# Soft-capped attention and two feed-forward layers on one core: the attention's blocks in batches of four

## The chip, the core and the metric

One core of one Trainium2 chip runs the whole program. Times are device microseconds (us) of one execution; a kernel's time is the median of its runs.

## The reference

Two batches of 12 heads, 448 positions, head width 64, all in fp32; then two feed-forward layers on the 896 rows of width 768.

```python
scores = (q @ k.T) / sqrt(64)
scores = cap * tanh(scores / cap)
attn = exp(scores - max(scores))
attn = attn / (sum(attn) + 1e-9)
x = attn @ v                               # 896 x 768 over heads
x = relu(x @ w_in) ** 2 @ w_out            # 768 -> 2048 -> 768
out = silu(x @ w2_in) @ w2_out
```

## The kernel before, in words

All products run on the matrix engine (PE), tanh and exp on ACT, sums and copies on DVE, some conversions on POOL. SP issues nearly all loads and stores. Every engine works through its own list in the order in which the program was written; the program is written by hand, and only semaphores hold an engine up.

**The attention** (`attention_bounded`, line 582) handles the 24 heads as 12 pairs, and two pairs (A and B) as a *quad* m, from 0 to 5. The 448 keys of a pair are three blocks of 128 and a rest of 64; the rests of A and B are put together in one block. So a quad has seven blocks, `A0 A1 A2 C B0 B1 B2`, where C is the block of rests, and there are 42 blocks in all. A block passes through:

- *scores* (`scores`, line 616): PE writes keys by queries for two heads into a pair of PSUM banks (`bank2`, two pairs in turn). ACT takes tanh out of it into a tile e, of which there are eight in turn (line 630); an exp in place follows (line 726). The pair of banks is free after the tanh.
- *values* (`values`, line 632): PE multiplies e with v and adds up in one bank per pair of heads, px.
- *add* (`add`, line 649): DVE adds the blocks of a pair to a tile total. The half of C that belongs to A is added when C comes, and B's half when B1 comes.

After B2, PE adds the totals up over the keys (`add_up`, line 663, into a bank `sum`); DVE copies them (`evacuate_sums`), SP moves them into another layout, DVE inverts them (`invert`, lines 693 and 694), SP stores them (line 695) and fetches them back, broadcast over the partitions (`fetch`, line 701), and DVE multiplies the copied px with them (`normalise`, line 706), after which POOL splits the result into two fp16 parts for the feed-forward. The last two pairs have another way: their sums are made on all partitions (`add_up_pair`, line 673) and inverted at full width (`last_sums`, line 709).

PSUM has eight banks: four for px, sums and what follows (`bank`), four as two pairs for scores.

**The order** is the loop from line 721 over batches `groups[h]` of two blocks, 21 of them. In iteration h come: the scores and tanhs of batch h, its exps, the loads that its blocks call for; the DVE copies of px that batch h-2 completed; adds and values of batch h-1; then, if batch h-2 had a B2, the sum of that quad and its copy. The rest of that quad's work hangs on a list `todo`: the inversion one iteration later, the fetch two, the two normalises four and six iterations later. Between iterations 5 and 16 one step per iteration prepares weights of the feed-forward (`ws.step`), and six weight loads stand at fixed iterations (`loads`, line 719).

**The feed-forward** follows at once. Its products (line 914) are ordered by a planner that interleaves the preparation of weights; its first products need the attention's pieces x0 in the order of the pairs. Its accumulators lie in the four banks that the scores had, and in the four others.

Of the kernel before, what the change touches and what calls it, by code (L numbers as in the profile page):

```python
# [8 lines left out]
F32 = mybir.dt.float32  # L9
BF16 = mybir.dt.bfloat16  # L10
# [5 lines left out]
ALU = mybir.AluOpType  # L16
# [10 lines left out]
def softcap_attention_relu2_silu(  # L27
# [48 lines left out]
    psum = ctx.enter_context(tc.tile_pool(name="psum", bufs=2, space=PSUM))  # L76

    dram = ctx.enter_context(tc.tile_pool(name="dram", bufs=1, space=bass.MemoryType.DRAM))

    def bank(name):  # L80
        return psum.tile([128, 512], F32, tag="p", bufs=4, name=name)

    def bank2(spool, name):
        return spool.tile([128, 2, 512], F32, tag="s", bufs=2, name=name)


    idle = work.tile([128, S], F32, tag="r", bufs=NR, name="idle")
    nc.vector.memset(idle[:, :128], 0.0)
    ib, ip = idle.bitcast(BF16), bank("idle")
    for _ in range(20):  # L90
        nc.tensor.matmul(ip[:, :256], lhsT=ib[:, :128], rhs=ib[:, :256], start=True, stop=True)


    cap = cap.rearrange("(a b) -> a b", a=1)
# [487 lines left out]
    def attention_bounded(att, spool, ws, x0):  # L582
# [22 lines left out]
        ex, total, px, sums, st, rb = {}, {}, {}, {}, {}, {}  # L605

        NQ = NP2 // 2
        blocks = [(m, x) for m in range(NQ) for x in ("A0", "A1", "A2", "C", "B0", "B1", "B2")]
# [1 line left out]
        def pair_of(m, x):  # L610
            return 2 * m + "AB".index(x[0])

        def head(j):
            return slice(64 * j, 64 * j + 64)

        def scores(m, x):
            sp = bank2(spool, f"s{m}_{x}")
            for j in range(2):
                for b in range(2) if x == "C" else (None,):
                    qk = pr.qk[pair_of(m, x) if b is None else 2 * m + b]  # L620
                    c = 3 if b is not None else int(x[1])
# [10 lines left out]
        def values(m, x):  # L632
            for i in (2 * m, 2 * m + 1) if x == "C" else (pair_of(m, x),):
                if i not in px:
                    px[i] = bank(f"px{i}")
            e = ex[m, x]
            for b in range(2) if x == "C" else (None,):
                for j in range(2):
                    i = pair_of(m, x) if b is None else 2 * m + b
                    v_m = pr.vt[i]  # L640
                    nc.tensor.matmul(  # L641
                        px[i][head(j), :S],
                        lhsT=v_m[:, 3 * j + int(x[1])] if b is None else pr.vc[m][head(b), j],
                        rhs=e[:, j] if b is None else e[head(b), j],
                        start=x == "A0" or b == 1,
                        stop=x == "B2" or b == 0,
                    )

        def add(m, x):
            e, i = ex[m, x], None if x == "C" else pair_of(m, x)  # L650
            if i == NP2 - 1:
                return
            if x in ("A1", "B1"):
                t = total[i] = att.tile([128, 2, S], F32, tag=f"total{x[0]}", bufs=2, name=f"total{i}")
                nc.vector.tensor_tensor(t, ex[m, x[0] + "0"], e, op=ALU.add)  # L655
            if x in ("A2", "B2"):
                nc.vector.tensor_tensor(total[i], total[i], e, op=ALU.add)  # L657
            if x in ("C", "B1"):
                b = int(x == "B1")
                t = total[2 * m + b][head(b)]  # L660
                nc.vector.tensor_tensor(t, t, ex[m, "C"][head(b)], op=ALU.add)  # L661

        def add_up(m):

            s = sums[m] = bank(f"sum{m}")
            for b in range(2):
                for j in range(2):
                    at = 32 * (2 * b + j)
                    nc.tensor.matmul(  # L669
                        s[at : at + 32, :S], lhsT=one[:, :32], rhs=total[2 * m + b][:, j], start=True, stop=True  # L670
                    )

        def add_up_pair(i, t, start=True, stop=True, part=slice(0, 128)):

            if start:
                sums["p", i] = bank(f"sump{i}")
# [28 lines left out]
        def normalise(i):  # L705
            nc.vector.tensor_tensor(cell(i), cell(i), rb.pop(i), op=ALU.mult)
            x0.now(i)
# [8 lines left out]
            return [a, b, c]  # L716

        todo, last = [], 2 * NQ - 2
        loads = {0: 0, 2: 1, 4: 2, 7: 3, 11: 4, 16: 5}
        groups = [blocks[n : n + 2] for n in range(0, len(blocks), 2)]  # L720
        for h in range(len(groups) + 1):
            if h < len(groups):
                for m, x in groups[h]:
                    scores(m, x)
                for m, x in groups[h]:
                    nc.scalar.activation(ex[m, x], ex[m, x], AF.Exp, scale=scale_c)  # L726
                for m, x in groups[h]:
                    if x in ("A0", "B0"):
                        i = pair_of(m, x)
                        if i + 2 < NP2:  # L730
                            pr.load_v(i + 2)
                    if x in ("A1", "C") and m + 1 < NQ:
                        pr.load(2 * m + 2 + (x == "C"))
            if h == 1:

                nc.vector.tensor_scalar(gcap, capt, -CAP_MAX, CAP_MAX, op0=ALU.max, op1=ALU.min)
                nc.scalar.activation(gcap, gcap, AF.Abs)
                nc.scalar.activation(gcap, gcap, AF.Exp, scale=-1.0)
                nc.vector.tensor_scalar(gcap, gcap, 1e-9 * ONE, None, op0=ALU.mult)
            older = groups[h - 2] if h > 1 else []  # L740
            for m, x in older:
                if x in ("C", "B2"):
                    evacuate(2 * m + (x == "B2"))
            for m, x in groups[h - 1] if h else []:
                add(m, x)
            for m, x in groups[h - 1] if h else []:
                values(m, x)
            for m, x in groups[h - 1] if h else []:
                if m == NQ - 1 and x in ("C", "B0", "B1", "B2"):
                    add_up_pair(  # L750
                        last + 1, ex[m, x], x == "C", x == "B2", head(1) if x == "C" else slice(0, 128)
                    )
                if m == NQ - 1 and x == "C":
                    add_up_pair(last, total[last])
            for m, x in older:
                if x == "B2":
                    add_up(m)
                    evacuate_sums(m)
                    todo.append((lambda m=m: invert(m), h + 1))
                    todo.append((lambda m=m: fetch(m), h + 2))  # L760
                    for b in range(2):
                        todo.append((lambda i=2 * m + b: normalise(i), h + 4 + 2 * b))
            if h in loads:
                ws.load_to(loads[h])
            for f, at in list(todo):
                if h >= at:
                    f()
                    todo.remove((f, at))
            if 5 <= h < 17:
                ws.step()  # L770
        for st_ in last_sums(last):
            st_.fn()
        for f, _ in todo:
            f()
        nc.scalar.activation(cell(last + 1), px.pop(last + 1)[:, :S], AF.Copy)
# [2 lines left out]
    def attention_general(att, spool, ws, x0):  # L778
# [8 lines left out]
        for i in range(NP2):  # L787
            pr.load(i)
            pr.load_whole_v(i)
            for j in range(2):  # L790
# [5 lines left out]
                    for a in ("mx", "nm", "sm", "rs")  # L796
                )
                for g in range(2):
                    sp = bank2(spool, f"sg{n}_{g}")
# [751 lines left out]
    def run(attention, tag, dt):  # L1551
        narrow = dt == F16
        power = POWER if narrow else dict.fromkeys(POWER, 0)
        with ExitStack() as pools:
# [96 lines left out]
```

## Time and profile before

| | |
|---|---|
| median of 3 runs | 499.09 us (498.02 to 499.17) |
| profiled execution | 498.42 us, of which the span from first to last instruction is 496.6 us |
| PE | 486.7 us busy, 98% |
| DVE | 404.5 us busy, 81% |
| ACT | 370.0 us busy, 75% |
| POOL | 31.2 us busy, 6% |
| PE's granted clock | 0.999 of full speed |
| chain that ended last | PE 94% |
| attention | from 5 us to 86.8 us of the span |

Busy time is the time in which an engine's instructions run. PE's is modelled at the ends, so 98% does not mean that its products run at their peak; that is why the lengths of single pieces and the waits are read below. The chain of work that ended last is followed back from the last instruction, at each step to what released it.

### The profile page before, as it was taken

Reading aid. Unit: us, or ns where it says so; the run is one execution under the profiler, and the core shown is the slowest. Engines: PE = TensorE matmul, PEld = TensorE weight load, DVE = VectorE, ACT = ScalarE, POOL = GpSimd, SP = SyncE. Lnnn points to the kernel's source line nnn. Section 1 sums busy time; section 2 is a strip of 40 time slices with the busy share of each in tenths; the row PEclk is TensorE's granted clock in tenths of the full one; section 3 lists DMA queues with packets and bytes.
Section 4 is the critical chain, followed back from the end, with each engine's and each line's share of the span. In section 5 each row is a group of like instructions: output and inputs, shape, how many; then the busy total and the mean of one; then the engine's idle time right before and its main releaser. Section 6 shows DMA issues by size and latency. Waiting matters only on the chain.

```text
span 496.6 us, 7168 instructions
## 1 busy us (share of the span) xinstructions
PE 486.7 (98%) x2581; PEld 235.1 (47%) x2581; DVE 404.5 (81%) x787; ACT 370.0 (75%) x594; POOL 31.2 (6%) x33
## 2 busy tenths in 40 slices
PE   8999999999999999999999998999999999998995
PEld 4323232555555555555555554555555555554552
DVE  0879998997987689967879967999876999988863
ACT  6999996999989995469998868778683589780200
POOL 1002455300000000000000000000000000000000
PEclk9999999999999999999999999999999999999999
DMA  7746562244544455374333211213573853033024
GB/s 249 275 150 182 170 178 60 103 131 128 191 162 156 147 180 182 129 276 169 127 128 127 66 63 65 88 41 127 177 261 117 279 163 118 1 100 124 0 77 154
DMA packets 22386, 69.76 MB, mean 140 GB/s; under 512 B 2886, under 2 KB 14150, under 8 KB 22342
## 3 DMA queue, kind: packets, MB, share of 16 engines
q1 hardware_dynamic: 22308, 69.22, 42.2%
q8 instruction: 22, 0.36, 0.3%
q14 instruction: 22, 0.18, 0.1%
q0 software_dynamic: 32, 0.00, 0.0%
q10 hardware_dynamic: 2, 0.00, 0.0%
HBM read 63.64 MB, written 5.54 MB: 139 GB/s over the span
## 4 chain that ended last, share of the span: by engine, by line
PE 94%; DVE 1%; ACT 1%; DMA 1%; issue 1%; SPq 1%; DVEq 0%
PE p_0df L914 8%; PE px L641 7%; PE p_6df L914 4%; PE yb_5f L914 4%; PE yb_2f L914 4%; PE yb_3f L914 4%; PE yb_1f L914 4%; PE yb_0f L914 4%; PE yb_4f L914 4%; PE s_B L622 3%; PE s_A L622 3%; PE ha_0f L914 3%; PE ha_1f L914 3%; PE p_4df L914 2%; PE c_0df L914 2%; PE ac10f L914 1%
## 5 line engine op out<-in xcount | busy, mean ns | idle before, releaser
L630 ACT ACTIVATE e_B<-s_B 128x896 f32<-128x896 f32 x18 | 15.9, 917 | 4.5 <-PE s_B L622 4.2
L630 ACT ACTIVATE e_A<-s_A 128x896 f32<-128x896 f32 x18 | 15.9, 918 | 3.5 <-PE s_A L622 3.3
L726 ACT ACTIVATE e_B<-e_B 128x896 f32<-128x896 f32 x18 | 16.5, 953 | 0.0
L726 ACT ACTIVATE e_A<-e_A 128x896 f32<-128x896 f32 x18 | 16.5, 955 | 0.0
L1283 DVE SCALAR_TENSOR_TENSOR yf<-p_6df,yf 128x448 f32<-128x448 f32 x15 | 9.2, 622 | 6.1 <-PE p_6df L914 6.1
L661 DVE TENSOR_TENSOR total<-total,e_C 64x896 f32<-64x896 f32 x11 | 12.9, 1174 | 0.4
L211 DVE SCALAR_TENSOR_TENSOR x1f<-yaf,x1f 128x448 f16<-128x448 f32 x12 | 7.4, 620 | 2.2 <-ACT x1f L853 2.1
L1283 DVE SCALAR_TENSOR_TENSOR yf<-p_4df,yf 128x448 f32<-128x448 f32 x15 | 9.0, 612 | 0.2 <-PE p_4df L914 0.2
L657 DVE TENSOR_TENSOR total<-total,e_A 128x896 f32<-128x896 f32 x6 | 8.8, 1471 | 0.3
L381 ACT ACTIVATE hl_103f<-u_84f 128x768 f16<-128x768 f32 x1 | 0.8, 845 | 9.5 <-DVE u_84f L406 9.5
L853 ACT ACTIVATE x1f<-yaf 128x448 f16<-128x448 f32 x12 | 6.7, 567 | 1.4 <-DVE yaf L864 1.3
L864 DVE TENSOR_TENSOR yaf<-yaf 128x448 f32<-128x448 f32 x12 | 7.1, 621 | 0.6 <-ACT yaf L853 0.5
L655 DVE TENSOR_TENSOR total<-e_A,e_A 128x896 f32<-128x896 f32 x6 | 6.6, 1102 | 0.6 <-ACT e_A L726 0.6
L655 DVE TENSOR_TENSOR total<-e_B,e_B 128x896 f32<-128x896 f32 x5 | 6.5, 1294 | 0.0
L714 DVE RECIPROCAL r<-r 128x448 f32<-128x448 f32 x2 | 5.9, 2953 | 0.1
L687 DVE COPY sm<-sum 128x448 f32<-128x448 f32 x5 | 3.1, 622 | 3.3 <-PE sum L669 3.3
L240 ACT ACTIVATE junk<-x0f 128x896 bf16<-128x896 f16 x6 | 5.7, 942 | 0.2
L657 DVE TENSOR_TENSOR total<-total,e_B 128x896 f32<-128x896 f32 x5 | 5.5, 1091 | 0.4
L726 ACT ACTIVATE e_C<-e_C 128x896 f32<-128x896 f32 x6 | 5.7, 954 | 0.0
L914 PE MATMUL p_4df<-yformsf,hl_92f 128*128 128x448 f16 x18 | 4.4, 352 | 1.3 <-DVE yf L1283 1.3
L630 ACT ACTIVATE e_C<-s_C 128x896 f32<-128x896 f32 x6 | 5.5, 924 | 0.0
L853 ACT ACTIVATE c_6df<-p_6df 128x448 f32<-128x448 f32 x3 | 1.6, 528 | 5.2 <-PE p_6df L914 5.2
(1862 smaller groups left out, 1648.1 us busy)
## 6 DMA issues: line engine op xcount, KB each, us to landing
yf<-spill SPq DMA_DIRECT2D x12, 224.0 KB, 4.8
out<-yf SPq DMA_DIRECT2D x12, 224.0 KB, 2.1
rb<-scratch SPq DMA_DIRECT2D x10, 224.0 KB, 3.9
raw_wb_0f<-in_moe_w_out SPq DMA_DIRECT2D x2, 768.0 KB, 6.9
raw_wb_1f<-in_moe_w_out SPq DMA_DIRECT2D x2, 768.0 KB, 4.1
raw_wb_2f<-in_moe_w_out SPq DMA_DIRECT2D x2, 768.0 KB, 4.3
raw_wb_3f<-in_moe_w_out SPq DMA_DIRECT2D x2, 768.0 KB, 4.3
raw_wb_4f<-in_moe_w_out SPq DMA_DIRECT2D x2, 768.0 KB, 4.9
```

The lines of the kernel that those rows point to most:

```text
L211: nc.vector.scalar_tensor_tensor(lo, x, scale, hi, op0=ALU.mult, op1=ALU.subtract, accum_out=watch.low() if see else None)
L622: nc.tensor.matmul(sp[:, j, :S] if b is None else sp[head(b), j, :S], lhsT=qk[head(j), 1, 128 * c : min(128 * c + 128, S)], rhs=qk[head(j) ...
L630: nc.scalar.activation(t, sp[:, :, :S], AF.Tanh, scale=scale_s)
L641: nc.tensor.matmul(px[i][head(j), :S], lhsT=v_m[:, 3 * j + int(x[1])] if b is None else pr.vc[m][head(b), j], rhs=e[:, j] if b is None els ...
L655: nc.vector.tensor_tensor(t, ex[m, x[0] + "0"], e, op=ALU.add)
L657: nc.vector.tensor_tensor(total[i], total[i], e, op=ALU.add)
L661: nc.vector.tensor_tensor(t, t, ex[m, "C"][head(b)], op=ALU.add)
L726: nc.scalar.activation(ex[m, x], ex[m, x], AF.Exp, scale=scale_c)
L853: return Step("A", cols, lambda: nc.scalar.activation(at(out), at(src), func, scale=scale), list(deps))
L864: return Step(eng, cols, lambda: e.tensor_tensor(at(out), at(x), at(y), op=op), list(deps))
L914: nc.tensor.matmul(acc, lhsT=w(e_w, kk), rhs=x(e_x, kk), start=first and i == 0, stop=last and i == len(n) - 1, skip_group_check=more,)
L1283: st = Step("D", S, lambda: nc.vector.scalar_tensor_tensor(yb, acc, to_y, yb, op0=ALU.mult, op1=ALU.add), list(deps))
```

## The change

The 42 blocks are handled in batches of 2, 2, seven times 4, and five times 2, 14 in all. Within a batch, C is moved to the end. The scores have three pairs of banks, each its own pool, used in turn; px has two banks. The sums take a half of a score pair; the sums of the last two pairs share one. The sum of a quad is written behind the values of the batch that holds its B2, one iteration earlier; its copy is at the head of the next iteration, ahead of the adds; inversion and fetch are both one iteration after that, the normalises two and three. The copy of a finished px is at the head of the iteration after its last block. The v loads stand behind the values. C's halves are added when both C and the pair's total exist. Weight loads and steps are tied to the number of the block and keep their places in the sequence of blocks to within a batch.

So the batches are, by number: 0 `A0 A1`; 1 `A2 C`; 2 `B0 B1 B2 A0`; 3 `A1 A2 B0 C`; 4 `B1 B2 A0 A1`; 5 `A2 B0 B1 C`; 6 `B2 A0 A1 A2`; 7 `B0 B1 B2 C`; 8 `A0 A1 A2 C`; 9 `B0 B1`; 10 `B2 A0`; 11 `A1 A2`; 12 `B0 C`; 13 `B1 B2`.

```diff
     def bank(name):
-        return psum.tile([128, 512], F32, tag="p", bufs=4, name=name)
+        pool, n = psum[-1]
+        return pool.tile([128, 512], F32, tag="p", bufs=n, name=name)
+    def next_banks(spools, name):
+        spools.append(spools.pop(0))
+        return bank2(spools[-1], name)
...
         def scores(m, x):
-            sp = bank2(spool, f"s{m}_{x}")
+            sp = next_banks(spool, f"s{m}_{x}")
...
         def add(m, x):
             e, i = ex[m, x], None if x == "C" else pair_of(m, x)
             if i == NP2 - 1:
                 return
+            for b in range(2) if x == "C" else ():
+                if 2 * m + b in total:
+                    rest_of(m, b)
...
-            if x in ("C", "B1"):
-                b = int(x == "B1")
-                t = total[2 * m + b][head(b)]
-                nc.vector.tensor_tensor(t, t, ex[m, "C"][head(b)], op=ALU.add)
+            added.add((m, x))
+            if x == "B1" and (m, "C") in added:
+                rest_of(m, 1)
...
         def add_up(m):
-            s = sums[m] = bank(f"sum{m}")
+            s = sums[m] = next_banks(spool, f"sum{m}")[:, 0]
...
-        loads = {0: 0, 2: 1, 4: 2, 7: 3, 11: 4, 16: 5}
-        groups = [blocks[n : n + 2] for n in range(0, len(blocks), 2)]
+        loads = {0: 0, 4: 1, 8: 2, 14: 3, 22: 4, 32: 5}
+        sizes = [2, 2] + [4] * 7 + [2] * 5
+        groups = [blocks[sum(sizes[:n]) : sum(sizes[: n + 1])] for n in range(len(sizes))]
+        groups = [sorted(gr, key=lambda e: e[1] == "C") for gr in groups]
+        first_late = next(n for n, gr in enumerate(groups) if {(NQ - 1, "C"), (NQ - 1, "B0")} & {*gr})
+        late_sums, lasting = [], spool[0]
         for h in range(len(groups) + 1):
+            if h == first_late + 1:
+                while spool[0] is not lasting:
+                    spool.append(spool.pop(0))
+                late_sums.append(next_banks(spool, "sums_late"))
...
-            older = groups[h - 2] if h > 1 else []
+            before, older = groups[h - 1] if h else [], groups[h - 2] if h > 1 else []
+            for i, n in list(left.items()):
+                if n == 0:
+                    evacuate(i)
+                    del left[i]
             for m, x in older:
-                if x in ("C", "B2"):
-                    evacuate(2 * m + (x == "B2"))
-            for m, x in groups[h - 1] if h else []:
+                if x == "B2":
+                    evacuate_sums(m)
+                    todo.append((lambda m=m: invert(m), h + 1))
+                    todo.append((lambda m=m: fetch(m), h + 1))
+                    for b in range(2):
+                        todo.append((lambda i=2 * m + b: normalise(i), h + 2 + b))
+            for m, x in before:
                 add(m, x)
-            for m, x in groups[h - 1] if h else []:
+            for m, x in before:
                 values(m, x)
+            for m, x in before:
+                if x in ("A0", "B0"):
+                    i = pair_of(m, x)
+                    if i + 2 < NP2:
+                        pr.load_v(i + 2)
...
-            for m, x in older:
-                if x == "B2":
+                if m < NQ - 1 and x == "B2":
                     add_up(m)
-                    evacuate_sums(m)
-                    todo.append((lambda m=m: invert(m), h + 1))
-                    todo.append((lambda m=m: fetch(m), h + 2))
-                    for b in range(2):
-                        todo.append((lambda i=2 * m + b: normalise(i), h + 4 + 2 * b))
...
-            if 5 <= h < 17:
-                ws.step()
-        for st_ in last_sums(last):
-            st_.fn()
+            ws.step(len({*here} & {*range(10, 34, 2)}))
+            if h == first_late + 1:
+                evacuate(last)
+                del left[last]
+                for st_ in last_sums(last):
+                    st_.fn()
...
-                tc.tile_pool(name=f"s{tag}", bufs=2, space=PSUM) as spool,
+                tc.tile_pool(name=f"p{tag}", bufs=2, space=PSUM) as ppool,
+                ExitStack() as banks,
             ):
-                attention(att, spool, ws, x0)
+                psum.append((ppool, 2 if narrow else 4))
+                spools = [
+                    banks.enter_context(tc.tile_pool(name=f"s{n_}{tag}", bufs=1 if narrow else 2, space=PSUM))
+                    for n_ in range(3 if narrow else 1)
+                ]
+                attention(att, spools if narrow else spools[0], ws, x0)
+            psum.append((pools.enter_context(tc.tile_pool(name=f"b{tag}", bufs=4, space=PSUM)), 4))
```

## Rows read from the trace of the kernel before

**Rows 1.** Chain that ended last, in order of time: start us, us, what.

```profile
11.24 1.70 PE s_B L622 x8
...
23.34 1.65 PE px L641 x8
...
59.65 0.91 PE s_C L622 x8
...
62.21 0.89 PE sum L669 x8
...
66.62 0.95 PE s_B L622 x4
67.58 0.75 PE s_A L622 x4
...
81.27 2.55 PE sump L678 x12
83.82 1.50 PE px L641 x8
...
86.83 4.65 PE ha_0f L914 x24
```

**Rows 2.** Waits of PE behind the attention, 86 to 497 us: total, times, longest.

```profile
PE ac0f L914 <- ACT u2c0f L853: 1.3, 1, 1.3
PE p_4df L914 <- DVE yf L1283: 1.3, 1, 1.3
```

**Rows 3.** Stretches: length; PE, weight loads, DVE, ACT, POOL busy; clock, DMA, GB/s.

```profile
16.00:26.00 10.00, 10.00 (x58) 3.00 (x56) 7.62 (x10) 10.00 (x13) 0.00 (x0) 1.00 0.62 208
...
37.17:51.82 14.65, 14.65 (x83) 4.60 (x82) 13.95 (x18) 13.63 (x17) 5.40 (x5) 1.00 0.72 198
```

**Rows 4.** Timeline of ACT, 5 to 90 us: start us, us, then the instruction.

```profile
6.05 1.73 ACT L630 ACTIVATE e_A<-s_A 128x896 f32<-128x896 f32 x2 [3.27 <-PE s_A L622]
...
12.97 1.71 ACT L630 ACTIVATE e_B<-s_B 128x896 f32<-128x896 f32 x2
...
19.52 1.74 ACT L630 ACTIVATE e_A<-s_A 128x896 f32<-128x896 f32 x2
```

**Rows 5.** Timeline of PE, 6.9 to 12 us; in brackets idle before and its end.

```profile
7.02 1.02 PE L622 MATMUL s_A<-qk0f 64*128 64x448 f32 x4 [0.27 <-ACT e_A L630]
```

**Rows 6.** Groups of DVE's instructions, 0 to 88 us: busy, mean ns | idle before.

```profile
L657 DVE TENSOR_TENSOR total<-total,e_A 128x896 f32<-128x896 f32 x6 | 8.8, 1471 | 0.3
...
L657 DVE TENSOR_TENSOR total<-total,e_B 128x896 f32<-128x896 f32 x5 | 5.5, 1091 | 0.4
...
L687 DVE COPY sm<-sum 128x448 f32<-128x448 f32 x5 | 3.1, 622 | 3.3 <-PE sum L669 3.3
...
L694 DVE RECIPROCAL st<-st 32x56 f32<-32x56 f32 x5 | 2.5, 491 | 0.2
L693 DVE TENSOR_SCALAR st<-st,gcap 32x56 f32<-32x56 f32 x5 | 1.3, 270 | 1.7 <-DMA st<-sm 1.7
...
L706 DVE TENSOR_TENSOR x_c4f<-x_c4f,rb 128x448 f32<-128x448 f32 x1 | 0.6, 606 | 0.0
```

**Rows 7.** SP's timeline, quad 1's store and fetch; the ten fetches to their landing.

```profile
42.16 0.33 SPq L695 DMA_DIRECT2D scratch<-st  x1
...
43.60 1.25 SPq L701 DMA_DIRECT2D rb<-scratch  x2
...
DMA to landing us min/median/max: 3.5/3.9/5.0
```

**Rows 8.** Timelines of DVE and PE: x0's last part, and the products that use it.

```profile
95.87 0.62 DVE L211 SCALAR_TENSOR_TENSOR x0f<-x_c11f,x0f 128x448 f16<-128x448 f32 x1
...
98.12 1.30 PE L914 MATMUL ha_1f<-x0f,hl_0f 128*128 128x448 f16 x6
```

**Rows 9.** Stretches after the last product, columns as in rows 3.

```profile
490.60:492.00 1.40, 0.07 (x1) 0.00 (x0) 0.62 (x1) 0.00 (x0) 0.00 (x0) 1.00 0.79 290
...
494.00:495.00 1.00, 0.00 (x0) 0.00 (x0) 0.00 (x0) 0.00 (x0) 0.00 (x0) 1.00 0.02 8
```

More of the change, by code (lines that the diff above doesn't have):

```diff
@@ L75, in softcap_attention_relu2_silu, with bank2 @@
     work = ctx.enter_context(tc.tile_pool(name="work", bufs=1))
-    psum = ctx.enter_context(tc.tile_pool(name="psum", bufs=2, space=PSUM))
     dram = ctx.enter_context(tc.tile_pool(name="dram", bufs=1, space=bass.MemoryType.DRAM))
+    psum = []
     def bank(name):
-        return psum.tile([128, 512], F32, tag="p", bufs=4, name=name)
-    def bank2(spool, name):
-        return spool.tile([128, 2, 512], F32, tag="s", bufs=2, name=name)
+        pool, n = psum[-1]
+        return pool.tile([128, 512], F32, tag="p", bufs=n, name=name)
+    def bank2(spool, name, n=1):
+        return spool.tile([128, 2, 512], F32, tag="s", bufs=n, name=name)
+    def next_banks(spools, name):
+        spools.append(spools.pop(0))
+        return bank2(spools[-1], name)
     idle = work.tile([128, S], F32, tag="r", bufs=NR, name="idle")
     nc.vector.memset(idle[:, :128], 0.0)
-    ib, ip = idle.bitcast(BF16), bank("idle")
-    for _ in range(20):
-        nc.tensor.matmul(ip[:, :256], lhsT=ib[:, :128], rhs=ib[:, :256], start=True, stop=True)
+    ib = idle.bitcast(BF16)
+    with tc.tile_pool(name="pi", bufs=1, space=PSUM) as ipool:
+        psum.append((ipool, 1))
+        ip = bank("idle")
+        for _ in range(20):
+            nc.tensor.matmul(ip[:, :256], lhsT=ib[:, :128], rhs=ib[:, :256], start=True, stop=True)
     cap = cap.rearrange("(a b) -> a b", a=1)
@@ L604, in attention_bounded @@
         scratch = dram.tile([NH, S], F32, tag="scratch", name="scratch")
-        ex, total, px, sums, st, rb = {}, {}, {}, {}, {}, {}
+        ex, total, px, sums, st, rb, left, added = {}, {}, {}, {}, {}, {}, {}, set()
         NQ = NP2 // 2
@@ L632, in values @@
         def values(m, x):
+            fresh, ended = {}, {}
             for i in (2 * m, 2 * m + 1) if x == "C" else (pair_of(m, x),):
-                if i not in px:
+                fresh[i] = i not in px
+                if fresh[i]:
                     px[i] = bank(f"px{i}")
+                left[i] = left.get(i, 4) - 1
+                ended[i] = left[i] == 0
             e = ex[m, x]
@@ L644, in values @@
                         rhs=e[:, j] if b is None else e[head(b), j],
-                        start=x == "A0" or b == 1,
-                        stop=x == "B2" or b == 0,
+                        start=fresh[i],
+                        stop=ended[i],
                     )
@@ L657, in add, with rest_of @@
                 nc.vector.tensor_tensor(total[i], total[i], e, op=ALU.add)
-            if x in ("C", "B1"):
-                b = int(x == "B1")
-                t = total[2 * m + b][head(b)]
-                nc.vector.tensor_tensor(t, t, ex[m, "C"][head(b)], op=ALU.add)
+            added.add((m, x))
+            if x == "B1" and (m, "C") in added:
+                rest_of(m, 1)
+        def rest_of(m, b):
+            t = total[2 * m + b][head(b)]
+            nc.vector.tensor_tensor(t, t, ex[m, "C"][head(b)], op=ALU.add)
         def add_up(m):
-            s = sums[m] = bank(f"sum{m}")
+            s = sums[m] = next_banks(spool, f"sum{m}")[:, 0]
             for b in range(2):
@@ L675, in add_up_pair @@
             if start:
-                sums["p", i] = bank(f"sump{i}")
+                sums["p", i] = late_sums[0][:, i - last]
             for j in range(2):
@@ L727, in attention_bounded @@
                 for m, x in groups[h]:
[L728 to L731, printed above, removed]
                     if x in ("A1", "C") and m + 1 < NQ:
@@ L739, in attention_bounded @@
                 nc.vector.tensor_scalar(gcap, gcap, 1e-9 * ONE, None, op0=ALU.mult)
-            older = groups[h - 2] if h > 1 else []
-            for m, x in older:
-                if x in ("C", "B2"):
-                    evacuate(2 * m + (x == "B2"))
-            for m, x in groups[h - 1] if h else []:
+            before, older = groups[h - 1] if h else [], groups[h - 2] if h > 1 else []
[3 more added lines that the diff above has]
+                    del left[i]
+            for m, x in older:
+                if x == "B2":
[5 more added lines that the diff above has]
+            for m, x in before:
                 add(m, x)
-            for m, x in groups[h - 1] if h else []:
+            for m, x in before:
                 values(m, x)
-            for m, x in groups[h - 1] if h else []:
+            for m, x in before:
[3 more added lines that the diff above has]
+                        pr.load_v(i + 2)
+            for m, x in before:
                 if m == NQ - 1 and x in ("C", "B0", "B1", "B2"):
                     add_up_pair(
-                        last + 1, ex[m, x], x == "C", x == "B2", head(1) if x == "C" else slice(0, 128)
+                        last + 1, ex[m, x], ("p", last + 1) not in sums, x == "B2", head(1) if x == "C" else slice(0, 128)
                     )
@@ L754, in attention_bounded @@
                     add_up_pair(last, total[last])
-            for m, x in older:
-                if x == "B2":
+                if m < NQ - 1 and x == "B2":
                     add_up(m)
-                    evacuate_sums(m)
-                    todo.append((lambda m=m: invert(m), h + 1))
-                    todo.append((lambda m=m: fetch(m), h + 2))
-                    for b in range(2):
-                        todo.append((lambda i=2 * m + b: normalise(i), h + 4 + 2 * b))
-            if h in loads:
-                ws.load_to(loads[h])
+            here = range(sum(sizes[:h]), sum(sizes[: h + 1]))
+            for n in here:
+                if n in loads:
+                    ws.load_to(loads[n])
             for f, at in list(todo):
@@ L798, in attention_general @@
                 for g in range(2):
-                    sp = bank2(spool, f"sg{n}_{g}")
+                    sp = bank2(spool, f"sg{n}_{g}", 2)
                     for e in range(2):
```

## The prediction

> **What bounds the kernel now.** I read the chain of work first, then the busy time by stretches, then the waits. The chain is the matrix engine (PE) nearly everywhere: through the attention its pieces follow each other without a gap up to 86.83 us, where the first feed-forward products begin [rows 1]. Behind that, PE waits only twice, 1.3 us each, on products far from the boundary [rows 2]. So a microsecond won or lost on PE in the attention moves the end by a microsecond.
>
> But PE is not alone. ACT, with its tanh and exp, is busy 10.00 of 10 us between 16 and 26, and between 37.17 and 51.82 PE has 14.65, DVE 13.95 and ACT 13.63 of 14.65 us [rows 3]. Whoever shortens PE's row there finds DVE and ACT a few per cent behind it.
>
> **What is removed.** A scores block that follows another kind of product takes 0.95 us, one right behind another scores block 0.75 (at 66.62 and 67.58 [rows 1]). A values block costs 0.90 and then 0.75: two take 1.65 (at 23.34), but 1.50 where products of the same shape stand ahead (at 83.82 [rows 1]). So a turn to scores costs 0.20 and a turn to values 0.15. A C block takes 0.91 wherever it stands [rows 1]; as its batch's last, it makes no second turn. 21 batches become 14: 7 x 0.35 = 2.45 us less. In the tail (sums of the last pair, 2.55 us now for C, total, B0, from 81.27 [rows 1]) the new order B0, C, total turns once more: +0.15. **Net -2.3.**
>
> **Three score pairs for four blocks.** The fourth block of a batch writes the pair that its own first block left, so it waits for that block's tanh. A pair comes back 0.97 us after its tanh starts: tanh at 6.05 [rows 4], the waiting scores at 7.02 [rows 5].
> Batch 2 (B0 B1 B2, A0 of quad 1) starts at 11.2 as now [rows 1], since ACT and the loads set the start; after three blocks PE is at 13.7. ACT starts these tanhs at 12.97 now [rows 4] and has no idle time to start earlier, so the pair is back at 14.0: 0.4 lost; with A0 and the values of A2 and C (0.90 + 0.91), 16.6.
> Batch 3 (A1 A2 B0 C): three scores take PE to 19.0. From 12.97 ACT owes the same four tanhs and four exps as now, 6.55 us until 19.52 [rows 4], so it reaches A1 at 19.6, and the pair is back at 20.6: **1.6 lost**. Now PE works on values in that time. C, four values blocks and sum 0 end at 25.6.
> From there a batch costs 3.20 or 3.36 for scores, 3.15 or 3.31 for values and 0.89 for a sum: batches 4 to 8 end at 32.1, 39.5, 46.0, 53.4 and 61.0. ACT needs some 6.6 per batch, and the first tanh of each is out before the fourth block asks, so I put these waits at nothing; if ACT were 0.3 slower per batch, they would cost that. Today's PE has done the same at 63.10 less two values blocks (1.65), 61.45 (sum at 62.21 [rows 1]). The early loss is just regained. Bounds of the two waits: 0 (ACT ahead) to 2.0; I take 2.0, since rows 3 show ACT full.
>
> **The sums move.** The sum of a quad now stands in the iteration that also adds its last block on DVE, where before a whole iteration lay between; and DVE normalises one or two iterations after the fetch, not two to four. DVE works in order, so a normalise that waits for its fetched row holds every add behind it. In batches of four this fits (6.5 us per iteration). In the five batches of two at the end it does not.
> Sum 3 leaves PE at 61.0. DVE then has its copy, 0.62, three adds (1.09 each, 1.47 with POOL at work; I take 1.2), the normalise of pair 3, 0.61, and the inversion of quad 2, 0.27 + 0.49 [rows 6]; with the two px copies that stand ahead (0.62 each, as the sum's copy), and a little queue, it is through at 67.4. The path to the broadcast row: 1.44 from the store's issue to the fetch's, 0.62 to the second half's, and 3.9 to land [rows 7]: 73.3. Only then come the normalise of pair 4, the inversion of quad 3 and the add of B2 of quad 4 (0.61 + 0.76 + 1.2): 75.9. PE stands at sum 4 at 61.0 + 5.0 + 3.35 + 3.35 = 72.7 (batches 9 to 11 score two blocks each, 1.70, ahead of the values of four, 3.31, and twice of two, 1.65). **Wait 3.2.** Bounds: without queue, adds at 1.09 and 3.5 to land, 1.6; adds at 1.47 and 5.0 to land, 5.4.
> The same once more: quad 3 is inverted at 74.7, its row lands at 80.6, and behind the normalise of pair 6 queue a px copy, the sum's copy, two adds, pair 7's normalise and C's add (0.61 + 0.62 + 0.62 + 2.4 + 0.61 + 1.2): 86.7. PE wants that total at 85.7: sum 4 until 76.8, batch 12's 3.5, and of the tail 1.70 + 1.81 + 0.90 + 0.89. **Wait 1.0**, bounds 0 and 2.0 (the adds and the landing at their ends).
>
> **Edits costed at nothing.** *SP:* the v loads move behind the values and the q and k loads forward; a load is issued a whole batch or more ahead of its use, over the 5.0 us that the slowest broadcast needed to land [rows 7]. Without that cover a batch starts late by the difference. The fetch, now in the inversion's iteration, holds SP for the store's 1.44, and loads behind it have the same cover. *Two values banks:* a finished bank is copied (0.62 [rows 6]) at the head of the next iteration, and is wanted after that iteration's scores; tightest in batch 9, with 1.5 us over. *Sums in a score pair:* its copy must be out before the batch's third block, 1.7 us; over this only if DVE runs late, bound 0.6 a time. *Pools:* the feed-forward's first accumulators take pairs whose tanh ended long before. *Feed-forward opening:* DVE arrives some 2 us later against PE; its last x0 part ends at 96.49 now (95.87 + 0.62) and is wanted 0.57 after 98.12 [rows 8], 2.2 us of cover; bounds 0 and 1.0, I take 0.
>
> **Sum:** -2.3 + 2.0 + 3.2 + 1.0 = **+3.9 us**. The profiled execution took 498.42; 502.3. The median of the runs shown, 499.09, stands 0.67 above it; I add nearly half: **502.6**.
>
> **Rivals.**
> *A, the waits are covered.* The fetched rows land in time, or DVE catches up, and of the waits only ACT's stays: -2.3 + 2.0 = -0.3, so 498.1. For it: no normalise waits today (idle 0.0 ahead of it [rows 6]). Against: the path alone needs 5.5 to 7 us, and iterations of two blocks last 3.35. Chance 0.17.
> *B, the turns decide: faster.* PE stays the only bound, ACT catching up before batch 3 and DVE before batch 10; then 498.42 - 2.3 = 496.1. The place is C's score in batch 3: if its pair is back by 19.0 PE never waits; the same for sum 4 at 72.7. Against: ACT's full row [rows 3]. The Trainium skill, page "TensorEngine Tiling (Array Packing)", section "Tiling Modes", says that changing the tiling mode drains the engine; by that rule alone this is the outcome, and rows 1 agree with the drain, at 0.15 to 0.20 us a turn. Chance 0.10.
> *C, worse than the sum: PE's clock falls in the wait at sum 4.* Then work behind it runs at 1.2 instead of 2.4 GHz for a while, and by estimate a stretch of 3 us would cost 3 more: 505.6. Against: after its last product PE idles from 490.67 and the granted clock is still 1.00 up to 495 [rows 9], longer than any wait here. The Trainium skill, page "TensorE: Matmul & The Clock Gate", section "HAM oscillation — how this bites in real kernels", has waits of PE throttle it so that the next work starts cold; by that rule it is this rival, and no row of this trace has it in the middle of work. Chance 0.05.
>
> **How the numbers follow.** My forecast has 0.68. What this kernel's measurement can tell from no change is 0.3%, 1.5 us: A is mostly "same" (0.15, the rest faster), B faster, forecast and C slower: 0.12, 0.15, 0.73. The forecast's own range by the bounds runs from 499.7 (1.6 and 0) to 505.5 (5.4 and 2.0). The asked one reaches down over A to 498.0 and up to 505.3, and leaves out B and the far end.
>
> **What would show it.** Right: first scores blocks of 0.95 only 14 times; PE idle 1.6 before the C block near 19; DVE idle ahead of a normalise near 71 to 73 and 77 to 80; PE waiting about 3 us at the sum, line 669 now, for a total on DVE; feed-forward starting near 90.7. Wrong: no DVE wait for a fetched row, PE without idle at 72 to 76, or ACT idle between 16 and 19.

## The result and the profile after

The change made the kernel slower: **506.61 us** (median of 4 runs, 505.84 to 507.00) against 499.13 for the kernel before beside it (4 runs), a ratio of 1.0148, 95% interval 1.0129 to 1.0168. The forecast, 502.6 us with a range up to 505.3, had the direction right, but the loss is twice as large: 7.5 us, where 3.5 were foretold.

| | before | after |
|---|---|---|
| profiled execution, us | 498.42 | 505.84 |
| its span, us | 496.6 | 503.5 |
| PE busy, us | 486.7 | 487.3 |
| DVE busy, us | 404.5 | 405.1 |
| ACT busy, us | 370.0 | 368.7 |
| first feed-forward product (PE's timeline), us | 86.76 | 93.05 |

No engine is busy for more than 0.6 us longer. The first feed-forward product comes 6.3 us later, the span is 6.9 us longer, and 0.5 us more lies around the span. So nearly all was lost inside the attention, by PE standing still and, for a stretch, working slowly.

The waits of PE (total us, times, longest); before, PE had no wait of this kind in the attention but 0.3 us at its start [rows 5]:

```profile
PE sum L688 <- DVE total L673: 2.9, 1, 2.9
...
PE s_C L631 <- ACT e_A L639: 1.3, 1, 1.3
PE s_A L631 <- DVE sm L706: 1.3, 1, 1.3
...
PE s_C L631 <- DMA qk1f<-in_k: 0.6, 1, 0.6
PE ha_1f L948 <- DVE x0f L220: 0.5, 1, 0.5
```

Those of DVE for a fetched row:

```profile
DVE x_c6f L725 <- DMA rb<-scratch: 3.6, 1, 3.6
DVE x_c4f L725 <- DMA rb<-scratch: 2.3, 1, 2.3
DVE x_c8f L725 <- DMA rb<-scratch: 2.1, 1, 2.1
DVE x_c0f L725 <- DMA rb<-scratch: 1.0, 1, 1.0
```

DVE waits 9.0 us in four places for a fetched row, where the normalise of before waited for nothing [rows 6]. The chain that ended last, nearly all PE there before [rows 1], now runs through those fetches:

```profile
71.55 3.90 DMA rb<-scratch
78.87 3.90 DMA rb<-scratch
91.93 4.65 DMA rb<-scratch
```

The timeline of DVE around sum 4 (start us, us, instruction, in brackets the idle time before and what ended it):

```profile
68.93 0.49 DVE L713 RECIPROCAL st<-st 32x56 f32<-32x56 f32 x1
...
72.11 1.09 DVE L680 TENSOR_TENSOR total<-total,e_C 64x896 f32<-64x896 f32 x1
75.53 0.62 DVE L725 TENSOR_TENSOR x_c4f<-x_c4f,rb 128x448 f32<-128x448 f32 x1 [2.33 <-DMA rb<-scratch]
76.08 0.23 DVE L712 TENSOR_SCALAR st<-st,gcap 32x56 f32<-32x56 f32 x1
76.34 0.49 DVE L713 RECIPROCAL st<-st 32x56 f32<-32x56 f32 x1
76.76 1.01 DVE L673 TENSOR_TENSOR total<-total,e_B 128x896 f32<-128x896 f32 x1
77.71 1.45 DVE L725 TENSOR_TENSOR x_c5f<-x_c5f,rb 128x448 f32<-128x448 f32 x1
```

Quad 2's sums are inverted by 69.4; their row is there at 75.5, and DVE has nothing else that it may do from 73.2 on. Behind the normalise of pair 4 queue the inversion of quad 3 and the last add of quad 4, which is ready at 77.8. The same time on PE:

```profile
20.31 0.59 PE L631 MATMUL s_C<-qk2f 64*64 64x448 f32 x1 [1.29 <-ACT e_A L639]
...
56.20 1.02 PE L631 MATMUL s_A<-qk8f 64*128 64x448 f32 x4 [1.27 <-DVE sm L706]
...
68.99 1.72 PE L654 MATMUL px<-e_B,vt9f 128*64 128x448 f32 x8
...
74.01 0.95 PE L688 MATMUL sum<-total,ones 128*32 128x448 f32 x4
77.83 0.95 PE L688 MATMUL sum<-total,ones 128*32 128x448 f32 x4 [2.88 <-DVE total L673]
78.71 1.47 PE L631 MATMUL s_B<-qk11f 64*128 64x448 f32 x4
...
81.81 2.08 PE L654 MATMUL px<-e_A,vt10f 128*64 128x448 f32 x8
...
93.05 2.44 PE L948 MATMUL ha_0f<-x0f,hl_0f 128*128 128x448 f16 x12
```

Sum 4 takes 4.70 us (74.01 to 78.71) in place of 0.89: its wait, and its two halves one after the other instead of side by side. And what follows is slow too: two values blocks take 2.08 where two took 1.72 at 68.99. Its cause is in the stretches (length; PE, weight loads, DVE, ACT, POOL busy; granted clock, DMA, GB/s):

```profile
79.00:80.00 1.00, 1.00 (x4) 0.01 (x2) 0.16 (x1) 0.00 (x0) 0.67 (x2) 0.57 0.08 32
80.00:81.00 1.00, 1.00 (x10) 0.30 (x8) 0.00 (x0) 0.78 (x1) 0.92 (x1) 0.50 0.88 283
81.00:82.00 1.00, 1.00 (x10) 0.19 (x4) 0.00 (x0) 0.19 (x2) 0.00 (x0) 0.50 0.60 143
82.00:83.00 1.00, 1.00 (x6) 0.27 (x6) 0.21 (x1) 1.00 (x2) 0.00 (x0) 0.72 0.00 0
83.00:84.00 1.00, 1.00 (x8) 0.29 (x6) 1.00 (x3) 1.00 (x2) 0.49 (x1) 1.00 0.00 0
```

PE's clock falls to 0.50 (1.2 of 2.4 GHz) behind the wait and is back by 83. Batch 12 takes 5.11 us (78.71 to 83.82).

### The profile page after: what moved, and what is told of

It reads as the page before. It is cut to its first block, busy times and chain, and to the rows that moved or that the text cites. A ratio compares the mean times of both kernels' runs of the same rounds, so it can differ in the third digit from the quotient of the medians.

```text
span 503.5 us, 7154 instructions
## 1 busy us (share of the span) xinstructions
PE 487.3 (97%) x2581; PEld 236.3 (47%) x2581; DVE 405.1 (80%) x787; ACT 368.7 (73%) x594; POOL 29.2 (6%) x33
## 4 chain that ended last, share of the span: by engine, by line
PE 79%; DVE 8%; DMA 6%; ACT 4%; issue 1%; SPq 1%; DVEq 0%
PE p_0df L948 7%; PE p_6df L948 4%; PE yb_0f L948 4%; PE yb_1f L948 4%; PE yb_4f L948 4%; PE yb_5f L948 4%; PE yb_2f L948 4%; PE yb_3f L948 4%; DMA rb<-scratch 4%; PE p_4df L948 2%; PE px L654 2%; PE c_0df L948 2%; PE ha_1f L948 2%; PE ac10f L948 1%; PE ac14f L948 1%
## 5 line engine op out<-in xcount | busy, mean ns | idle before, releaser
L671 DVE TENSOR_TENSOR total<-e_A,e_A 128x896 f32<-128x896 f32 x6 | 9.2, 1533 | 0.0
L688 PE MATMUL sum<-total,ones 128*32 128x448 f32 x40 | 5.7, 551 | 2.9 <-DVE total L673 2.9
L673 DVE TENSOR_TENSOR total<-total,e_A 128x896 f32<-128x896 f32 x6 | 7.2, 1194 | 0.5
L948 PEld LDWEIGHTS <-hl_0f 128*128 128x128 f16 x36 | 3.4, 98 | 4.5 <-issue 1.5
```

The costliest lines, as they stand in the source:

```text
L948: nc.tensor.matmul(acc, lhsT=w(e_w, kk), rhs=x(e_x, kk), start=first and i == 0, stop=last and i == len(n) - 1, skip_group_check=more,)
```

## The experiments

Three theories stood against each other. **O, the order:** DVE holds its queue at a normalise whose row is still under way; sum 4's wait and the fall of the clock follow. **V, the volume:** DVE is too full, whatever the order. **P, the banks:** three score pairs and two values banks are the cost.

**The normalises one iteration later (norm_later).** The smallest undoing of O's cause.

```diff
-                        todo.append((lambda i=2 * m + b: normalise(i), h + 2 + b))
+                        todo.append((lambda i=2 * m + b: normalise(i), h + 3 + b))
```

> Both normalises of a quad come one iteration later (three and four behind the copy of its sum, not two and three); nothing else differs. Theory O (order): DVE is held at line 725 by a row that has not landed, the add of B2 of quad 4 queues behind it, and PE waits 3.8 us at sum 4 and then works 1.6 us slower at a lower clock. By O the wait at sum 4 falls to 1 us or less, DVE's waits for rb fall from 9.0 us to under 3, the clock stays at 1.00, the feed-forward starts near 88 (now 93.05), and the time is 501.5 (500.5 to 502.5). Theory V (volume): DVE is simply too full for a batch's adds to be done in their own iteration; then the wait at sum 4 stays over 3 us and the time at 505 or more. Theory P (banks): three pairs and two values banks are what costs; then the time stays at 506 too.

Measured 499.34 us (10 runs), a ratio to before of 1.0008 (0.9996 to 1.0020). DVE's waits for rows fall from 9.0 to 1.9 us, and PE's timeline has sum 4 in 1.30 us (72.50 to 73.80). The copy of sum 2 is no longer waited for either, which the expectation had not counted on; so the time lies below O's range, 500.5 to 502.5.

```profile
72.50 1.37 PE L688 MATMUL sum<-total,ones 128*32 128x448 f32 x8
73.80 1.02 PE L631 MATMUL s_B<-qk11f 64*128 64x448 f32 x4
...
77.32 1.77 PE L631 MATMUL s_B<-qk11f 64*128 64x448 f32 x8
```

Batch 12 takes 3.52 us here, so the fall of the clock cost after's 5.11 some 1.6. One number in one line gives back nearly all of the loss: O holds; V and P can't be the main cost, since volume and banks are as after.

**Batches of four to the end (fours_to_end).** The other way to give the row time: long iterations.

```diff
-        sizes = [2, 2] + [4] * 7 + [2] * 5
+        sizes = [2, 2] + [4] * 9 + [2]
```

> The five batches of two at the end become two of four and one of two (2, 2, nine times 4, 2). Theory O: the wait for a fetched row costs PE only where an iteration is short; with iterations of 6.5 us there is no wait at sum 4, no fall of the clock, and two turns fewer, 0.7 us: feed-forward at about 87, time 500.5 (499.5 to 501.5). The wait of batch 8's third scores block for the copy of a sum stays, about 1.3. Theory V: the same adds on a DVE that is too full, so PE still waits 3 us or more at the sums and the time is 504 or more. Theory P: more batches of four, more waits for pairs; 507 or more.

Measured 509.01 us, 1.0207 (1.0181 to 1.0234): a miss. Sum 4's wait is gone, but quad 4's row now comes too late for the feed-forward. DVE waits 6.2 us for it in one piece, and these are PE's waits:

```profile
PE ha_1f L948 <- DVE x0f L220: 1.9, 1, 1.9
...
PE ha_0f L948 <- POOL x0f L1511: 1.2, 1, 1.2
PE ha_1f L948 <- ACT x0f L887: 1.2, 1, 1.2
...
PE ha_0f L948 <- POOL x0f L1512: 1.0, 1, 1.0
```

PE waits 5.3 us for pieces of x0 in place of 2.9 at the sum, and behind these waits its clock falls too, to 0.50 from 107 to 110. The time is one that P allowed (507 or more), and waits for a score pair did rise: the copies of sums cost 1.3 and 1.1, and one more wait for ACT 0.8. But the feed-forward starts at 88.74, 4.3 us earlier than in after; most of the loss comes behind it. It is O's stall in another place: the twos at the end are there for the last quad.

**PE kept busy during the wait (busy_pe).** Between the halves of sum 4, 14 products of a total that is long ready, into the unused half of its pair of banks; nothing reads them.

```diff
             for b in range(2):
+                for n in range(14 if (m, b) == (4, 1) else 0):
+                    nc.tensor.matmul(
+                        pair[32 * (n % 4) : 32 * (n % 4) + 32, 1, :S],
+                        lhsT=one[:, :32], rhs=total[2 * m][:, n % 2], start=True, stop=True,
+                    )
                 for j in range(2):
```

> Between the two halves of sum 4, PE makes 14 more products of the total of pair 8 into the unused half of the same pair of banks, 14 times 0.22 us, 3.1 us of work inside the wait of 3.8 us; their results are not used. If it is PE's idle time that lets its clock fall (0.50 between 80 and 82), the clock stays at 1.00, batch 12 costs 3.5 us and not 5.1, and the time is 505.1 (504.7 to 505.7), 1.3 to 1.6 us under the changed kernel. If batch 12 is slow for another reason, the time stays at 506.6 or rises.

Measured 506.02 us, 1.0147 (1.0130 to 1.0164), above the expected 504.7 to 505.7: a miss in the time. The stretches behind the sum:

```profile
79.00:80.00 1.00, 1.00 (x12) 0.21 (x8) 0.00 (x0) 0.45 (x1) 0.91 (x2) 1.00 0.47 161
80.00:81.00 1.00, 1.00 (x12) 0.34 (x6) 0.00 (x0) 0.98 (x2) 0.69 (x1) 1.00 1.00 251
```

And a wait of PE that after doesn't have:

```profile
PE sums_late L703 <- DVE total L680: 1.2, 1, 1.2
```

The clock stays at 1.00 and batch 12 takes 3.52 us (78.48 to 82.00): PE's idleness is what let it fall. But the time hardly moves, because PE now arrives at the last total before DVE has it: the second wait of my sum, foretold at 1.0, was hidden behind the slow clock. The feed-forward starts at 92.46, 0.59 us earlier than after's, and 0.23 of that was there at the start of batch 12 (78.48 against 78.71). So the clock's 1.6 us were worth 0.4, and the medians can't be told apart.

**The copy of the sum ahead of the copies of px (copy_first).** For the wait of 1.3 at 56.20: the two loops at the head of an iteration change places.

```diff
-            for i, n in list(left.items()):
-                if n == 0:
-                    evacuate(i)
-                    del left[i]
             for m, x in older:
                 if x == "B2":
                     evacuate_sums(m)
...
+            for i, n in list(left.items()):
+                if n == 0:
+                    evacuate(i)
+                    del left[i]
```

> At the head of an iteration DVE copies the sum out of its score pair before it copies finished px banks. By theory O the pair comes back 0.54 us earlier: PE's wait at the third scores block of batch 8 falls from 1.27 to 0.7 us and the time by 0.5, to 506.1 (505.6 to 506.7). If that wait is not for the copy, nothing changes; if a values bank is now late, PE waits at line 654 and the time rises.

Measured 506.58 us, 1.0155 (1.0126 to 1.0184). That wait falls from 1.3 to 0.9 us, sum 4's is 3.0, and the whole doesn't move. DVE comes late to the copy because it is late altogether. Why it is late there shows beside norm_later. In after, POOL splits the first early normalise's result from 45.76 and prepares a weight behind it, and DVE's add beside these is long:

```profile
48.00 1.93 DVE L671 TENSOR_TENSOR total<-e_A,e_A 128x896 f32<-128x896 f32 x1
48.92 1.94 POOL L361 CAST zeros<-raw_wa2f 128x768 f16<-128x768 bf16 x1
```

The same add in norm_later, whose POOL had prepared that weight at 38.43:

```profile
47.42 1.08 DVE L671 TENSOR_TENSOR total<-e_A,e_A 128x896 f32<-128x896 f32 x1
```

With the next add (1.71 against 1.09) and one conversion (1.38 against 0.53) that is 2.3 us, and DVE copies sum 2 at 55.53 in after, at 53.33 in norm_later. A wait for a row isn't needed for it: busy_pe had none before this place, and PE still waited 0.6 us for the copy. That it is POOL's work which makes the adds long is read from the overlap, not tried by itself.

**Early normalises in the kernel before (before_early).** O's cause put alone into a kernel with batches of two and with the old banks.

```diff
-                    todo.append((lambda m=m: fetch(m), h + 2))
+                    todo.append((lambda m=m: fetch(m), h + 1))
                     for b in range(2):
-                        todo.append((lambda i=2 * m + b: normalise(i), h + 4 + 2 * b))
+                        todo.append((lambda i=2 * m + b: normalise(i), h + 2 + b))
```

> The kernel before, with nothing changed but that the fetch of the inverted sums is one iteration after the sum and the normalises two and three after it (as they are written after the change), in place of two, four and six. The broadcast row needs about 5.9 us from DVE's inversion to landing and an iteration has 3.35, so DVE stands some 2.5 us in each of the five quads ahead of the first normalise. Theory O: the stall holds the adds behind it; the sum stands an iteration later here, which gives 3.35 us of slack, so PE loses only where DVE is full (37 to 52 us): 499.5 to 502. Theory V (DVE is simply too full, whatever the order): the same work in another order, no change, 498.5 to 499.5.

Measured 514.98 us, 1.0327 (1.0304 to 1.0351): the direction of O, far above its range. Two of DVE's waits in its timeline:

```profile
51.90 0.62 DVE L706 TENSOR_TENSOR x_c2f<-x_c2f,rb 128x448 f32<-128x448 f32 x1 [3.35 <-DMA rb<-scratch]
...
100.35 0.62 DVE L706 TENSOR_TENSOR x_c8f<-x_c8f,rb 128x448 f32<-128x448 f32 x1 [7.47 <-DMA rb<-scratch]
```

PE's timeline at the two sums that wait:

```profile
54.81 1.00 PE L669 MATMUL sum<-total,ones 128*32 128x448 f32 x4 [2.92 <-DVE total L657]
...
85.29 0.94 PE L669 MATMUL sum<-total,ones 128*32 128x448 f32 x4 [1.98 <-DVE total L657]
```

A stretch behind each, with the clock at 0.50:

```profile
57.00:58.00 1.00, 1.00 (x4) 0.34 (x2) 0.90 (x2) 0.35 (x1) 1.00 (x1) 0.50 0.10 37
...
87.00:88.00 1.00, 1.00 (x6) 0.60 (x4) 0.97 (x1) 0.02 (x1) 1.00 (x2) 0.50 0.00 0
```

DVE waits 16.6 us in five places. I had counted 2.5 each with an iteration of slack at the sums; the slack is used up at quads 2 and 4 (2.9 and 2.0), the clock falls after both, the feed-forward starts at 96.9, and there PE waits another 4.5 us for x0, with the clock at 0.50 once more behind it (114 to 117). Batches of four aren't needed for the loss.

**All batches of two, with norm_later's normalises (twos).** What stays is banks, sum and fetch.

```diff
-        sizes = [2, 2] + [4] * 7 + [2] * 5
+        sizes = [2] * 21
```

> Normalises one iteration later, and all batches of two blocks: what stays of the change is the three score pairs and two values banks, the sum in the iteration of its last add, and the fetch beside the inversion. The turns come back (+2.45 against norm_later) and the wait at the C block near 20 goes (-1.3). Theory O (order of DVE): with iterations of 3.35 us the sum that follows its last add at once waits for DVE in the middle quads, where DVE has 13.95 of 14.65 us of work; about 1 to 2 us more, so 501 to 503. If the sum's early place costs nothing in itself, 499.1 to 500.5.

Measured 503.89 us, 1.0113 (1.0088 to 1.0138), 4.6 above norm_later and 0.9 above O's range. PE's timeline at sum 3:

```profile
63.23 0.94 PE L688 MATMUL sum<-total,ones 128*32 128x448 f32 x4 [2.48 <-DVE total L673]
```

And the stretch behind it, with the clock at 1.00:

```profile
64.00:65.00 1.00, 1.00 (x6) 0.30 (x4) 1.00 (x4) 0.00 (x0) 0.00 (x0) 1.00 0.95 278
```

The sum stands in the iteration of its last add; when that iteration has 3.35 us, PE is there before DVE. PE waits 2.7 us at sums, and counted as for sum 4 (the halves one after the other) sums 1 and 3 cost 1.2 and 3.4 us. With the turns (2.45), without the wait for ACT (1.3) and norm_later's 0.4 at sum 4, and with a start 0.6 better, that is 4.8 of the 4.95 us by which the feed-forward starts later (91.50 against 86.55). Four blocks per batch don't only save turns, they pay for the early sum. Whether the banks alone cost anything wasn't tried by itself.

**The block of rests in its place (c_in_order).** On top of norm_later.

```diff
-        groups = [sorted(gr, key=lambda e: e[1] == "C") for gr in groups]
```

> Normalises one iteration later (as in norm_later), and the block of rests left where it stands in the order of the blocks, not moved to the end of its batch. This prices that part of the change alone. By the price of a turn (0.20 to scores, 0.15 to values) each C block in the middle of a batch of four makes one turn more in the scores and one in the values, in the three or four batches where it isn't already last: 0.35 a batch, so 1.0 to 1.4 us longer than norm_later: 500.3 to 500.7. If the turn costs only what DVE and ACT leave over, or the order of the adds matters as much (C's halves are then added earlier and the sum's total is ready earlier), nothing or a gain of up to 0.4: 498.9 to 499.3.

Measured 499.29 us (12 runs), 1.0011 (0.9999 to 1.0024), against norm_later's 1.0008: no difference that can be measured, where the price of a turn had led me to expect 1.0 to 1.4 us. Where C stands inside a batch of four, its scores take 3.57 us (32.15 to 35.72) in place of norm_later's 3.37 (31.83 to 35.20), and the values with it 3.47 in place of 3.32: the turns cost what the prediction took, 0.20 and 0.15. But only two batches have C inside in the order of the blocks (at the ends of others it makes no second turn), not the three or four that I counted, and in the first of them the wait for ACT is 0.14 shorter. The feed-forward starts at 86.96 in place of 86.55. C last in its batch is a small part of the change.

**Batches of three early on (threes).** On top of norm_later.

```diff
-        sizes = [2, 2] + [4] * 7 + [2] * 5
+        sizes = [2, 2] + [3] * 4 + [4] * 4 + [2] * 5
```

> Normalises one iteration later (as in norm_later), and the first of the batches of four made shorter: 2, 2, four times 3, four times 4, five times 2. In norm_later PE still loses 1.3 us at the C block near 20 (waiting for ACT's tanh of the block three earlier), some 0.4 at sum 4 and 0.3 at the start. If the wait at the C block comes from a fourth score block that wants a pair while ACT is still behind its early tanhs (the theory of the prediction), batches of three, which fit in three pairs, do without it, at one turn more (0.35): a net gain of about 1.0 to 1.3 us against norm_later, so about 498.1 to 498.4 and a little below before. If the wait is only ACT's backlog, whatever the batch, PE waits the same 1.3 us in other places and the time is 499.3 to 499.7.

Measured 499.96 us (12 runs), 1.0024 (1.0012 to 1.0036): a miss. The wait for ACT at the C block is gone, as foreseen, but PE's timeline has new ones:

```profile
20.75 0.94 PE L688 MATMUL sum<-total,ones 128*32 128x448 f32 x4
21.87 0.94 PE L688 MATMUL sum<-total,ones 128*32 128x448 f32 x4 [0.18 <-DVE total L673]
22.75 1.77 PE L631 MATMUL s_B<-qk3f 64*128 64x448 f32 x8
...
55.80 1.02 PE L631 MATMUL s_A<-qk8f 64*128 64x448 f32 x4 [0.64 <-DVE sm L706]
```

Sum 0 takes 2.00 us in place of 0.89, right behind its last add. The first tanh also came 1.5 us later in this execution than in norm_later's, so the size of that wait isn't safe; the median rests on all 12.

**Mixed sizes (mixed).** On top of norm_later: four where a quad ends early on, threes behind it.

```diff
-        sizes = [2, 2] + [4] * 7 + [2] * 5
+        sizes = [2, 2, 4, 3, 3, 3, 3, 3, 4, 4, 3, 2, 2, 2, 2]
```

> Normalises one iteration later, and batches of 2, 2, 4, five times 3, 4, 4, 3, four times 2: 15 batches. The batch that ends a quad early on is one of four (batch 2, as in norm_later), so that sum 0 doesn't ask for its total at once as it did in threes (1.1 us lost there), and the next is one of three, so that no fourth block waits for ACT (1.3 us in norm_later). If each wait belongs to its place, and there is room for both, PE loses under 0.6 us to sum 4 and the copies of sums; 15 batches save 2.1 us of turns less 0.15 in the tail and 0.3 at the start: about 1.3 us below before, 497.3, ratio 0.997. If DVE and ACT are so full that a wait taken away at one place comes back at another, 498.3 to 499.5, and a new wait of PE on DVE (a total or a copy of a sum) or on ACT stands in the trace.

Measured **497.54 us** (10 runs), a ratio of 0.9978 (0.9968 to 0.9987): 0.2% faster than before, and some 9 us faster than after. All of PE's waits outside the start:

```profile
PE ac0f L948 <- ACT u2c0f L887: 1.3, 1, 1.3
...
PE p_4df L948 <- DVE yf L1317: 0.9, 1, 0.9
PE s_A L631 <- ACT e_B L639: 0.8, 1, 0.8
```

DVE never waits for a row, PE waits once in the attention, and the feed-forward starts at 85.91, 0.85 us earlier than before (86.76).

**Mixed sizes, rests in place (mixed_in_order).** On top of c_in_order, with sizes 2, 2, 4, 3, 3, 3, 3, 4, 4, 4, 2, 2, 2, 2, 2.

```diff
-        sizes = [2, 2] + [4] * 7 + [2] * 5
+        sizes = [2, 2, 4, 3, 3, 3, 3, 4, 4, 4, 2, 2, 2, 2, 2]
```

> The block of rests left in its place (as in c_in_order), normalises one iteration later, and batches of 2, 2, 4, four times 3, three times 4, five times 2: 15 batches. c_in_order showed that the block's place makes no difference of more than 0.3 us to the whole with batches of four. If that holds for other sizes too, it comes out as mixed within 0.5 us: 497.0 to 497.8 if the waits stay away, 498.3 to 499.5 if they come back elsewhere.

Measured 498.50 us (11 runs), 0.9986 (0.9973 to 0.9998), in the range given for waits that come back elsewhere. The feed-forward starts at 86.00, as in mixed, but then waits 0.9 us for x0, behind a DVE that waited 2.0 for quad 4's row.

## Why the prediction was right in kind and wrong in size

The mechanism was the one foretold: a normalise that waits for its row holds the adds, and PE stands at sum 4. Term by term, in us of PE's time until the feed-forward (93.05 less 86.76 is 6.3):

| term | forecast | after |
|---|---|---|
| turns, with the tail | -2.3 | -2.3 (what the others leave) |
| start | 0 | +0.2 |
| waits for ACT, batches 2 and 3 | +2.0 | +1.4 |
| copy of sum 2, batch 8 | 0 | +1.5 |
| sum 4 | +3.2 | +3.8 |
| clock at half behind it | 0 | +1.6 |
| last total | +1.0 | 0 |

- **Three score pairs for four blocks** held: the C block waited 1.3 at 20.3 (foretold 1.6 near 19), batch 2 0.1 (0.4), with the start 0.2 late, where qk1 landed late for the C block.
- **The sums move** held in place and cause. Sum 4 was 0.6 longer than taken, inside its bounds: the wait in batch 8 put PE and DVE off alike, by 1.3, and DVE's first add behind sum 3 took 1.92 beside POOL, where I took 1.2. (DVE's list behind sum 3 adds up to 67.8, not the 67.4 that I wrote, which makes the term 3.6; and the last total was wanted at 85.6, not 85.7.) The second wait, 1.0, is 0 in this trace, since the total was there at 88.9 and PE only at 89.14; busy_pe showed that it was covered by the slow clock, not absent.
- **Edits costed at nothing, "Sums in a score pair"** is the first step that failed. I bounded the copy at 0.6 a time and took 0; in batch 8 the third score block waited 1.27 and paid a turn again, 1.5 in all. The condition was written down ("over this only if DVE runs late"), but I judged DVE's lateness from the end of the attention alone; rows 3 had it at 13.95 of 14.65 us just before, and what POOL's work beside its adds does there was left out. The feed-forward's opening, costed at 0 with 1.0 as the bound, cost 0.5.
- **Rival C came on top of the forecast**, at a chance of 0.05, and that is the second step that failed. I dismissed it because the clock stays at 1.00 through PE's idle end [rows 9]. A stretch after the last product didn't show what happens to work that follows a wait. The Trainium skill, page "TensorE: Matmul & The Clock Gate", section "HAM oscillation — how this bites in real kernels", says that waits throttle PE and the next work starts cold; after's trace agrees, at 0.50 from 80 to 82; twos does not, at 1.00 behind a wait of 2.48. The rival's price was 3 us; it was 1.6, and net 0.4, since DVE had to be waited for anyway.

Forecast 3.9, of which 1.0 didn't come; 1.5 and 1.6 came unforeseen, 0.6 more at sum 4, 0.6 less at ACT, 0.2 at the start: 6.2. Most of the rest up to the medians' 7.5 is the feed-forward's wait and the 0.5 around the span. The range was too narrow by the prediction's own bounds: its far end, 505.5, counts those of sum 4 and of the last total alone. With the 0.6 of one copy and the 1.0 of the opening it would have been 507.1, and the clock was in none of them.

Rival A (waits covered, 498.1) was what a different line would have given: norm_later, at 499.34, is nearly it. Rival B would need ACT ahead as well; mixed comes closest, at 0.9978.

## What to carry to other kernels

Where an engine works in order, place the consumer of a slow round trip by the time that the trip takes (here 6 us from inversion to landing), not by a count of iterations: the same offset that costs DVE 1.0 us at most in after's iterations of 6.5 us stalls it by 2.3 and 3.6 in iterations of 3.35. The end of the work needs its own look: fours_to_end has long iterations, and its last row still came 6.2 us late. When turns of the busiest engine are saved, read how far the next engines are behind it in the same stretch, since a producer moved next to its consumer has lost its slack. When one wait is removed, look for the next one behind it before counting its whole length as gain.

## What the runs showed of the hardware that was not expected

The granted clock falls in the middle of work, and the length of the wait alone doesn't decide it. It fell to 0.50 after waits of 2.88 us (after, sum 4), 2.92 and 1.98 (before_early, sums) and 3.0 (copy_first, sum 4), also behind the waits for x0 in before_early (3.8 and 0.7) and fours_to_end (1.0 to 1.9, four in a row), and each time it stood there for some 3 us. It stayed at 1.00 after a wait of 2.48 (twos, sum 3) and over the idle end of the kernel before [rows 9]. What sets these apart is open. A normalise on DVE took 1.45 us beside POOL (77.71 in after), 0.62 without it; the add just ahead of it (76.76), beside the same POOL instruction, took 1.01 and was not longer than others.
